# Causal masks moved from TensorE into the decay rows, another order of the query chunks, and float16 halves for part of one product

## The chip, the cores and the metric

The kernel runs on one core of a Trainium2 chip. The metric is device time in microseconds (us), as the median of three runs. A core has TensorE (PE in the profile; PEld is its weight load), VectorE (DVE), ScalarE (ACT), GpSimd (POOL) and SyncE (SP), which issues all DMAs here. Each engine takes its instructions in the order in which the program holds them, and waits on semaphores for the others.

## What is computed

Attention with a decay, then two feed-forward layers. The reference, cut:

```
scores = (1/8) * q @ k.T                           # 4 batches, 8 heads, 576 positions, 64 wide
cum    = cumsum(log(clip(f, 1e-4, 1)))
scores = where(causal, -1e9, scores + cum[:, None] - cum[None, :])
attn   = softmax(scores) @ v                       # -> x, 2304 tokens x 512
h = x @ w_in;   x = (h * sigmoid(h)) @ w_out       # layer 1, 512 -> 2048 -> 512
h = x @ w2_in;  x = (h * cos(h)) @ w2_out          # layer 2, the same sizes
```

Layer 1's `(g @ w_out)` is the "second product" below.

## The kernel before

**Tiling.** Tokens go through the layers in nine blocks of 256 (`NB`), the hidden width in eight pairs of 128 (`NPR`). One (layer, block, pair) is a step. Layer 1 takes 72 steps, layer 2 another 72. A step is 24 matmuls of the first product (tile `h`, line 1086), an elementwise chain, and the second product (tile `y`; line 1186 in layer 1 with 24 matmuls, line 989 in layer 2 with 21). Every product is computed from operands split into a high and a low half, with three matmuls of halves (`PASS`) for one full one. `h` takes float16 halves, scaled by a power of two for each operand; layer 1's `y` takes halves in fp32r (the 32-bit format that TensorE rounds), without scales; layer 2's `y` takes scaled float16 halves.

**Attention.** Positions 0 to 255 are done by 16 jobs of kind `a` (unit `c01`), positions 256 to 575 by 16 jobs of kind `b` with three units: `c2` (rows 256 to 383, 384 keys wide), `c3` (rows 384 to 511, 512 wide) and `T` (the last 64 rows of both heads, 576 wide). A unit computes its scores in PSUM (`f_s`), adds the decay row and takes the row maximum on VectorE (`top`, line 649: one operation adds the row to the scores, scales by -1/8 and keeps the minimum), exponentiates on ScalarE, normalises, transposes on TensorE (line 686) and ends in one value product for the job (line 766). The decay rows (`jb.dk`, one copy of a head's row in all 128 partitions, and `jb.dt` for `T`) come by DMA. The causal mask of a diagonal chunk is a matmul with the identity that opens the accumulation: line 632 for `c2` and `c3` (two of 128x128 in each unit), line 621 for `T` (one of 128x64), line 629 for `c01`.

**Blocks and jobs.** Blocks 0 to 3 need the jobs `a`; blocks 4 to 7 the chunks `c2` and `c3` of one batch each; block 8 all the `T` rows. So the steps of blocks 0 to 3 run between the jobs `b`.

**Weights.** All weights arrive as 64-bit words and are rebuilt on GpSimd, ScalarE and VectorE (`convert`, lines 429 to 442). `w1i` is then scaled and split into float16 (`chi` and `clo`), `w1o` split into fp32r. A scale (`scale_tasks`) is the sum of squares (ACT), one addition (DVE), a matmul with one column (line 380) and four one-column operations (DVE, lines 385 to 388).

**What sets the order.** The program is not written in the order in which it runs. Every piece is a task with an engine, a modelled duration, dependencies, buffers to acquire and a key; the `Scheduler` plays a model of the engines and emits whichever ready task has the lowest key. Steps have keys near -1000 (on PE the transposes, scores and value products of attention come ahead of them), the `a` and `b` jobs 0 to about 150, layer 1's weights 4 to about 50, and layer 2's weights 150 and up. The order that comes out is fixed in the program.

Of the kernel before, what the change touches and what calls it, by code (L numbers as in the profile page):

```python
# [43 lines left out]
W2N0, W2N1 = 16, 1.4  # L44
QA, QB = 768, 1600
# [223 lines left out]
def decay_attention_silu_cos_kernel(ctx, tc, qa, qb, f, w1i, w1o, w2i, w2o, out):  # L269
# [10 lines left out]
    w2_d = {("i", c): dr.tile([128, 2, 512], F16, name=f"w2i_d{c}") for c in range(NF)}  # L280
    w2_d.update({("o", p, k): dr.tile([128, 2, 512 if k < 3 else 256], F16, name=f"w2o_d{p}_{k}") for p in range(NPR)
# [40 lines left out]
    maskt = sb.tile([128, 64], BF16, name="maskt")  # L322
# [13 lines left out]
    rg2 = sb.tile([128, NPR], F32, name="rg2")  # L336
    v2 = sb.tile([128, 2, NPR], F32, name="v2")
    vm = sb.tile([128, 4], F32, name="vm")
    ry2 = sb.tile([128, NB], F32, name="ry2")
# [28 lines left out]
    SW = lambda l, kind, p: 2 * NB + (0 if l == 1 else NPR if kind == "i" else 2 * NPR) + p  # L368
# [143 lines left out]
    def load_tasks(jb, u):  # L512
# [45 lines left out]

        def decays():
# [37 lines left out]
        if beta:  # L597
            r.append(add("SP", 1.0, decayt, [t1], key=u, dma=c_dma(0.29), name="ldd"))
        return r

    def unit_tasks(jb, kind, pos, split, rel):
# [12 lines left out]
        def f_s():  # L614
# [5 lines left out]
            if tail:  # L620
                mm(st[1][:, 256:320], identb, maskt, start=True, stop=False, skip_group_check=True)
                for n, (x, y) in enumerate(PASS):
                    mm(st[0][:, 0:256], jb.tail[x], jb.k[y][:, 0:256], start=n == 0, stop=n == 2, skip_group_check=True)  # L623
                    mm(st[1][:, 0:320], jb.tail[x], jb.k[y][:, 256:S], start=False, stop=n == 2, skip_group_check=True)  # L624
                return
            for a in range(2):
                if kind == "c01":
# [3 lines left out]
                else:  # L631
                    mm(st[a][:, w - 128:w], identb, mask, start=True, stop=False, skip_group_check=True)
            if kind == "c01":
# [8 lines left out]
            for n, (x, y) in enumerate(PASS):  # L642
                for a in range(2):
                    r = slice(64 * a, 64 * a + 64)
                    mm(st[a][:, 0:w], jb.q[x][r, c:c + 128], jb.k[y][r, 0:w], start=False, stop=n == 2, skip_group_check=True)  # L645
# [71 lines left out]
        pe = {"c01": 0.9, "c2": 0.66, "c3": 0.8, "T": 0.86}[kind]  # L717
        ts = add("PE", pe, f_s, split + [masked], key=i - 10000.0, acq=["s", "s"] + ["e"] * heads + ["su"], rel=rel, name="S")
        te = []
        for a in range(2):  # L720
            d = {"c01": 0.78, "T": (0.45, 0.52)[a]}.get(kind, c_dve(w) + 0.15)
            t = add("DVE", d, lambda a=a: f_max(a), [ts] if not (tail and a) else [ts, t], key=i + 0.1 * a, rel=["s"], name="max")
            if not tail or a:
                h = 0 if tail else a
                te.append(add("ACT", (0.9 if kind == "c01" else c_act(w) + 0.19), lambda h=h: f_exp(h), [t], key=i + 0.1 * h,
                              name="exp"))
        tr = add("DVE", 0.3, f_rec, te, key=i, name="rec")
        r = []
        for a in range(heads):
            tn = []  # L730
            for j, (o, n) in enumerate(((0, 128), (128, 256)) if kind == "c01" else ((0, w),)):
                k = 2 * a + j if kind == "c01" else a
                def nf(eng, a=a, o=o, n=n, k=k):
# [5 lines left out]
                    acq=["s"] * (2 if tail else 1) + (["pt"] if kind in ("c01", "c2") and a == 0 else []), rel=["e"],  # L739
# [56 lines left out]
    for kind, b in ORDER:  # L796
        if kind == "a":
            pos += {1: GAP4, 2: GAP8}.get(b, 0)
        for hp in range(H // 2):
# [26 lines left out]
    MK = -1000.0  # L826

# [74 lines left out]
    xready, factor, last_out = {}, {}, {}  # L902
# [32 lines left out]
    def factor_tasks(l, j, ts, key):  # L935
# [12 lines left out]
        if l == 2:  # L948
            t = add("DVE", 0.4, f2, [ts, factors2], key=key, name="sc")
            return [t] * NPR  # L950
        wts = [wready[1, "i", 2 * p][0] for p in range(NPR)]
# [92 lines left out]
    for l, j, p in order:  # L1044
# [59 lines left out]
        if l == 1:  # L1104
# [11 lines left out]
            def half(i, s=(l, j, p)):  # L1116
                if s not in g_t:
                    g_t[s] = sbt("g", [128, 2, 2 * TB], F32R)
                return g_t[s][:, i]

# [3 lines left out]
            t3 = add(**copies(lambda half=half: half(0), src, 512, ("ACT", "DVE"), half_r), deps=[t2], key=k_el, acq=["g"],  # L1124
                     name="g")
            t4 = add(**rest(lambda half=half: half(1), src, half_r, lambda half=half: half(0).bitcast(F32), 512),
# [44 lines left out]
        prev = None  # L1171
        wdeps = [t for i in range(2) for t in wready[l, "o", 2 * p + i]]
# [89 lines left out]
```

## Time and profile before

| | |
|---|---|
| device time, median of 3 runs (lowest to highest) | 983.35 us (982.35 to 983.75) |
| the profiled execution | 983.18 us, of which the span from first to last instruction is 981.3 us |
| PE busy | 955.5 us, 97% of the span |
| DVE busy | 757.2 us, 77% |
| ACT busy | 628.0 us, 64% |
| POOL busy | 123.2 us, 13% |
| mean granted TensorE clock | 0.991 |

Busy time is an average over stages: start-up with weight conversion and the `a` jobs (to about 165 us), the `b` jobs among layer 1's steps (to about 420 us), the rest of layer 1 (to about 625 us), layer 2. Matmuls overlap in the records, so the mean duration of one (about 275 ns) is not its pace; the pace is read from the chain that ended last, where a piece of 24 matmuls stands with the time from its start to the start of the next piece.

### The profile page before, as it was taken

Reading aid. Unit: us, or ns where it says so; the run is one execution under the profiler, and the core shown is the slowest. Engines: PE = TensorE matmul, PEld = TensorE weight load, DVE = VectorE, ACT = ScalarE, POOL = GpSimd, SP = SyncE. Lnnn points to the kernel's source line nnn. Section 1 sums busy time; section 2 is a strip of 40 time slices with the busy share of each in tenths; the row PEclk is TensorE's granted clock in tenths of the full one; section 3 lists DMA queues with packets and bytes.
Section 4 is the critical chain, followed back from the end, with each engine's and each line's share of the span. In section 5 each row is a group of like instructions: output and inputs, shape, how many; then the busy total and the mean of one; then the engine's idle time right before and its main releaser. Section 6 shows DMA issues by size and latency. Waiting matters only on the chain.

```text
span 981.3 us, 20944 instructions
## 1 busy us (share of the span) xinstructions
PE 955.5 (97%) x8223; PEld 826.4 (84%) x8223; DVE 757.2 (77%) x1792; ACT 628.0 (64%) x1219; POOL 123.2 (13%) x157
## 2 busy tenths in 40 slices
PE   7996899999999999999999999999999999999997
PEld 4475688887888878889999999988888888888886
DVE  4999976677879888858778742678888888878875
ACT  6896866577776768745455432676766766766663
POOL 4865320011111121200000000000000000000000
PEclk9998899999999999999999999999999999999999
DMA  8575234435566575334433338500010001000000
GB/s 305 182 267 195 92 108 154 157 118 177 174 208 186 181 224 189 102 115 146 167 125 125 108 128 255 193 23 23 23 44 23 23 23 44 1 23 1 23 22 22
DMA packets 55906, 115.27 MB, mean 117 GB/s; under 512 B 8128, under 2 KB 18368, under 8 KB 55808
## 3 DMA queue, kind: packets, MB, share of 16 engines
q1 hardware_dynamic: 55808, 113.94, 35.0%
q8 instruction: 64, 1.05, 0.4%
q14 instruction: 34, 0.28, 0.1%
HBM read 89.20 MB, written 24.72 MB: 116 GB/s over the span
## 4 chain that ended last, share of the span: by engine, by line
PE 89%; DVE 7%; issue 1%; ACT 1%; POOL 1%; POOLq 0%; DVEq 0%; ACTq 0%
PE h L1086 37%; PE y L1186 20%; PE y L989 17%; PE pv L766 4%; PE tt L686 4%; PE st L645 3%; DVE rw L438 2%; DVE w L442 1%; DVE wi L306 1%; PE st L638 1%; PE dp L584 1%; PE st L624 1%; PE st L623 1%; DVE e L649 1%; DVE wo L300 1%
## 5 line engine op out<-in xcount | busy, mean ns | idle before, releaser
L1086 PE MATMUL h<-x,wi 128*128 128x256 f16 x3456 | 412.2, 274 | 3.1 <-ACT wi L286 1.7
L1086 PEld LDWEIGHTS <-wi 128*128 128x128 f16 x3456 | 330.0, 98 | 52.7 <-issue 6.1
L1186 PE MATMUL y<-g,wo 128*128 128x256 f32 x1728 | 238.2, 290 | 4.4 <-ACT g L286 3.6
L1186 PEld LDWEIGHTS y<-g,wo 128*128 128x128 f32 x1728 | 216.4, 192 | 11.9 <-issue 6.1
L989 PE MATMUL y<-wo,g 128*128 128x256 f16 x1512 | 176.3, 273 | 0.0
L989 PEld LDWEIGHTS <-g 128*128 128x128 f16 x1512 | 148.0, 98 | 17.1
L669 ACT ACTIVATE e<-e,su 128x128 f32<-128x128 f32 (+4 forms) x144 | 82.9, 577 | 22.5 <-DVE su L649 20.8
L1135 ACT ACTIVATE t<-h,ru 128x512 f32<-128x512 f32 x72 | 49.4, 686 | 67.3 <-PE h L1086 67.1
L1111 ACT ACTIVATE t<-h,rg 128x512 f32<-128x512 f32 x72 | 49.3, 685 | 64.1 <-PE h L1086 62.7
L1158 DVE TENSOR_TENSOR g<-t,g 128x896 f16<-128x896 f32 x72 | 78.4, 1089 | 8.7 <-ACT g L1155 5.2
L649 DVE CUSTOM_DVE_ANT_0 e<-st,dk 128x256 f32<-128x256 f32 (+3 forms) x144 | 64.1, 478 | 23.8 <-PE st L645 13.4
L288 POOL TENSOR_SCALAR e<-e,su 128x128 f32<-128x128 f32 (+4 forms) x68 | 50.7, 751 | 247.5 <-DVE su L676 135.4
L1145 DVE SCALAR_TENSOR_TENSOR t<-h,rg,t 128x512 f32<-128x512 f32 x72 | 53.9, 749 | 31.8 <-ACT t L1142 31.8
L306 DVE SCALAR_TENSOR_TENSOR g<-t,rg,g 128x512 fp32r<-128x512 f32 x72 | 55.3, 769 | 28.8 <-ACT g L286 28.2
L1141 ACT ACTIVATE t<-t,ru 128x512 f32<-128x512 f32 x72 | 51.7, 718 | 39.9 <-DVE t L1138 39.9
L1114 DVE SCALAR_TENSOR_TENSOR t<-t,h 128x512 f32<-128x512 f32 x72 | 49.2, 683 | 35.0 <-ACT t L1111 34.5
L1155 ACT ACTIVATE g<-t 128x896 f16<-128x896 f32 x72 | 67.5, 938 | 5.0 <-DVE t L1151 5.0
L286 ACT ACTIVATE g<-t,rg 128x512 fp32r<-128x512 f32 x49 | 35.3, 721 | 53.3 <-PE y L1186 50.0
L1138 DVE SCALAR_TENSOR_TENSOR t<-t,ru,h 128x512 f32<-128x512 f32 x72 | 53.5, 743 | 20.4 <-ACT t L1135 19.9
L286 ACT ACTIVATE pt<-tt 128x384 f32<-128x384 f32 (+2 forms) x90 | 44.5, 518 | 23.5 <-PE tt L686 23.1
L686 PE MATMUL tt<-ident,e 128*128 128x128 f32 x384 | 55.7, 275 | 3.4 <-POOL e L288 2.8
L1142 ACT ACTIVATE t<-t,halfpi 128x512 f32<-128x512 f32 x72 | 52.0, 722 | 2.3
(128 smaller groups left out, 1146.7 us busy)
## 6 DMA issues: line engine op xcount, KB each, us to landing
rw<-w1i SPq DMA_DIRECT2D x16, 512.0 KB, 5.2
rw<-w1o SPq DMA_DIRECT2D x16, 512.0 KB, 6.8
x<-x_d SPq DMA_DIRECT2D x16, 512.0 KB, 3.9
dk<-decay_d SPq DMA_DIRECT2D x16, 512.0 KB, 4.2
raw<-w2i SPq DMA_DIRECT2D x16, 512.0 KB, 4.9
raw<-w2o SPq DMA_DIRECT2D x16, 512.0 KB, 4.4
qs<-qb SPq DMA_DIRECT2D x16, 480.0 KB, 4.6
w2o_d<-w SPq DMA_DIRECT2D x24, 256.0 KB, 2.1
```

The source lines that it names most:

```text
L286: nc.scalar.activation(dst, src, AF.Copy, scale=scale)
L306: fn=lambda: nc.vector.scalar_tensor_tensor(out(), a(), scale(), b(), ALU.mult, ALU.subtract))
L649: nc.vector.tensor_tensor_reduce(out, s, d, -0.125, first, ALU.add, ALU.min, cell["sm"][:, o:o + 1])
L669: nc.scalar.activation(x, x, AF.Exp, bias=sm[:, i:i + 1], scale=-1.0, accum_out=sm[:, 4 + i:5 + i])
L686: nc.tensor.transpose(tt[a][:, 128 * c:128 * c + 128], e[a][:, 128 * c:128 * c + 128], ident)
L989: nc.tensor.matmul(y[bank][:, 256 * half:256 * half + 256], g[:, gi, ga], w[:, wi, 256 * col:256 * col + 256], start=p == 0 and half == 0 ...
L1086: nc.tensor.matmul(h[:, i], w[:, wi, 128 * k:128 * k + 128], x[:, xi, k], start=(i == 0 and q == 0 and k == 0), stop=(i == 1 and q == 2 an ...
L1138: nc.vector.scalar_tensor_tensor(cell["t"], cell["t"], r, cell["h"], ALU.subtract, ALU.subtract)
L1145: nc.vector.scalar_tensor_tensor(cell["t"], cell["h"], r, cell["t"], ALU.mult, ALU.mult)
L1155: nc.scalar.activation(g_t[s][:, 0], cell["w"], AF.Copy)
L1158: nc.vector.tensor_tensor(g_t[s][:, 1], cell["w"], g_t[s][:, 0], ALU.subtract)
L1186: nc.tensor.matmul(y[:, e * TB:(e + 1) * TB], w[:, wi, 128 * ec:128 * ec + 128], g[:, gi, i * TB:(i + 1) * TB], start=(st and e == 0), sto ...
```

## The change

Three edits in one.

*Masks.* For `c2`, `c3` and `T` the mask matmuls go. GpSimd writes the fill value into the masked part of the decay rows themselves by `affine_select` (`hide`): for `c3` columns 384 to 511 of both heads' rows, for `T` the last 64 columns of each half, and for `c2` columns 256 to 383. The two chunks share one set of rows, and `c3` needs columns 256 to 383 whole. So the units run as `c3`, `c2`, `T`, and the select for `c2` depends on both maxima of `c3`. The small tile `maskt` and its two copies go.

*Float16 for the second product.* From block index 3 (`J16 = 3`, the fourth of nine) layer 1's `y` takes scaled float16 halves: 48 of 72 steps. The fp32r halves of `w1o` are still made for blocks 0 to 2; from them a second set is made (squares, scales per pair, `chi`, then `left` and `low` on DVE), stored to DRAM (`w1_d`) and loaded over the fp32r set in pair p once block 2's step p has been multiplied. The factors are in `f_v1` (`rg3`) and `f3` (`ry1`), which the elementwise chain and the eviction of `y` apply.

*Keys.* The new weight tasks have keys 80 to 87, behind the `a` jobs and amid the `b` jobs.

```diff
+J16, C16 = 3, 80.0
...
-        nc.gpsimd.tensor_copy(maskt[0:64], mask[0:64, 0:64])
-        nc.gpsimd.tensor_copy(maskt[64:128], mask[64:128, 64:128])
...
+        def hide(kind):
+
+            def f():
+                if kind == "T":
+                    for a in range(2):
+                        d = jb.dt[64 * a:64 * a + 64, 512:S]
+                        nc.gpsimd.affine_select(out=d, in_=d, pattern=[[-1, 64]], compare_op=ALU.is_ge, fill=NEG, base=0,
+                                                channel_multiplier=1)
+                    return
+                c = 128 * int(kind[1])
+                d = jb.dk[:, :, c:c + 128]
+                nc.gpsimd.affine_select(out=d, in_=d, pattern=[[0, 2], [-1, 128]], compare_op=ALU.is_ge, fill=NEG, base=0,
+                                        channel_multiplier=1)
+            return f
...
+            jb.masked = {"c3": [add("POOL", 0.6, hide("c3"), [t1], key=u, name="hide")],
+                         "T": [add("POOL", 0.7, hide("T"), [td], key=u, name="hide")]}
...
-                mm(st[1][:, 256:320], identb, maskt, start=True, stop=False, skip_group_check=True)
...
-                else:
-                    mm(st[a][:, w - 128:w], identb, mask, start=True, stop=False, skip_group_check=True)
...
+        if kind == "c3":
+            jb.masked["c2"] = [add("POOL", 0.6, jb.hide("c2"), tm, key=i, name="hide")]
...
-                for i, u in enumerate(("c2", "c3", "T")):
+                for i, u in enumerate(("c3", "c2", "T")):
...
+    for p in range(NPR):
+        k, key = SW(1, "o", p), C16 + p
...
+        q = [add(**squares(lambda c=c, hi=hi: hi(c), 512, sq[:, c % 2, k:k + 1]), deps=wready[1, "o", c], key=key, name="sqw")
+             for c in pair]
+        ts = scale_tasks(k, q, key, 14)
...
+                nc.vector.scalar_tensor_tensor(st["w"], hi(c), scl[:, k:k + 1], st["t"][:, 0], ALU.mult, ALU.subtract)
...
+                nc.vector.scalar_tensor_tensor(st["t"][:, 1], lo(c), scl[:, k:k + 1], st["w"], ALU.mult, ALU.add)
...
+            w1_done[c] = add("SP", 0.46, lambda st=st, c=c: nc.sync.dma_start(w1_d[c], st["t"]), [t6], key=key, rel=["w16"],
+                             dma=c_dma(0.26), name="w2d")
...
+        if j == J16:
+            for c in (2 * p, 2 * p + 1):
+                def load16(c=c):
+                    wo_t[c] = sb.tile([128, 2, 1024], F16, tag=f"wo{c}", bufs=1, name="wo")[:, :, 0:512]
+                    nc.sync.dma_start(wo_t[c], w1_d[c])
+                wready[1, "o", c] = [add("SP", 0.46, load16, [w1_done[c], out_done[J16 - 1, p]], key=k_in - 2, dma=c_dma(0.26),
+                                         name="w2l")]
```

What it does to the order of instructions is shown at three places; in the rows `st` are scores, `e` exponentials, `su` maxima and sums, `one` and `qk` the mask's identity and the queries and keys, and the numbers tell buffers apart.

TensorE, the scores of a unit `c2` before (the second of its two masks first):

```order
L632 MATMUL st_2203<-one_133 128x128
L632 LDWEIGHTS one_133
L632 MATMUL st_2204<-one_133 128x128
L645 MATMUL st_2203<-qk_1955 128x384
L645 MATMUL st_2204<-qk_1955 128x384
```


and the scores of a unit `c3`, which now comes first, after a step's `y`:

```order
L1267 MATMUL y_1550<-g_2447,wo_1725 128x256 x6
L1267 MATMUL y_1551<-g_2447,wo_1676 128x256 x6
L1267 MATMUL y_1551<-g_2447,wo_1725 128x256 x6
L662 MATMUL st_2675<-qk_2315 128x512
L662 MATMUL st_2676<-qk_2315 128x512
```


The mask's loads and matmuls are gone, and the scores follow the step's matmuls at once.

VectorE, where the last pair of `w1i` tiles is finished (`wi`), before:

```order
L306 SCALAR_TENSOR_TENSOR wi_1734<-w_1578,scl_143,wi_1734 128x512
L940 TENSOR_SCALAR rg1_145<-inv_144 128x1 x2
L306 SCALAR_TENSOR_TENSOR wi_1732<-w_1501,scl_143,wi_1732 128x512
L288 TENSOR_SCALAR xo_1765<-pv_1725 128x256
L306 SCALAR_TENSOR_TENSOR g_1759<-t_1700,rg1_145,g_1759 128x512
L649 ISA e_1776,su_1773<-st_1774,dk_1540 128x128
L649 ISA su_1773 128x1
L649 ISA e_1776,su_1773<-st_1774,dk_1540 128x256
```


and now:

```order
L308 SCALAR_TENSOR_TENSOR wi_1777<-w_1560,scl_158,wi_1777 128x512
L1180 SCALAR_TENSOR_TENSOR t_1789<-t_1789,h_1719 128x512
L308 SCALAR_TENSOR_TENSOR wi_1787<-w_1640,scl_158,wi_1787 128x512
L870 SCALAR_TENSOR_TENSOR w_1819<-wo_444,scl_158,w16_1754 128x512
L873 SCALAR_TENSOR_TENSOR w16_1745<-wo_436,scl_158,w_1771 128x512
L873 SCALAR_TENSOR_TENSOR w16_1754<-wo_444,scl_158,w_1819 128x512
L308 SCALAR_TENSOR_TENSOR g_1827<-t_1789,rg1_160,g_1827 128x512
L387 TENSOR_SCALAR inv_159<-nrm_1779 128x1
L388 TENSOR_SCALAR inv_159<-inv_159 128x1
L389 TENSOR_SCALAR scl_158<-inv_159 128x1
L390 TENSOR_SCALAR inv_159<-scl_158 128x1
```


Behind the last `wi`, where the maxima of an attention unit stood, now stand the new weight operations (lines 870 and 873) and scale chains (lines 387 to 390). The steps' own operations (`t`, `g`) keep their places; at the 20th pass of the operation that was line 1114 the order held 88 of the 160 maxima before and holds 70 now, and all 16 new weight tiles are done by then.

GpSimd, among the `b` jobs, before:

```order
L288 TENSOR_SCALAR e_2919<-e_2919,su_2915 128x384
L288 TENSOR_SCALAR e_2961<-e_2961,su_2958 128x512
L288 TENSOR_SCALAR e_3087<-e_3087,su_3084 128x384
L288 TENSOR_SCALAR e_3088<-e_3088,su_3084 128x384
L288 TENSOR_SCALAR raw_3209<-raw_3209 128x512
L288 TENSOR_SCALAR e_3326<-e_3326,su_3323 128x384
L288 TENSOR_SCALAR raw_3321<-raw_3321 128x512
```


and now:

```order
L290 TENSOR_SCALAR e_2716<-e_2716,su_2712 128x384
L567 AFFINE_SELECT dk_2633<-dk_2633 64x64 x2
L572 AFFINE_SELECT dk_2633<-dk_2633 128x2x128
L290 TENSOR_SCALAR qk_2962<-qs_2702 128x960
L290 TENSOR_SCALAR raw_2883<-raw_2883 128x512
L290 TENSOR_SCALAR e_2900<-e_2900,su_2897 128x512
L572 AFFINE_SELECT dk_2958<-dk_2958 128x2x128
```


The selects stand in one queue with the normalisations of `e` and with the conversion of layer 2's weights (`raw`).

## Rows read from the trace of the kernel before

**Rows 1.** Busy time by stretch, us; (x) counts instructions; PEclk is the granted clock.

```profile
core 0: us, PE busy (x) PEld busy (x) DVE busy (x) ACT busy (x) POOL busy (x), PEclk, DMA share, GB/s
80.00:105.00 25.00, 15.23 (x88) 12.24 (x86) 24.27 (x67) 16.21 (x37) 9.04 (x12) 0.73 0.54 197
105.00:230.00 125.00, 124.36 (x1064) 104.43 (x1065) 93.21 (x267) 85.73 (x209) 21.16 (x29) 1.00 0.42 134
230.00:420.00 190.00, 190.00 (x1609) 158.14 (x1609) 154.50 (x439) 138.34 (x304) 32.90 (x40) 1.00 0.55 174
420.00:625.00 205.00, 204.97 (x1796) 192.27 (x1797) 135.58 (x309) 92.03 (x170) 6.62 (x8) 1.00 0.47 156
625.00:975.00 350.00, 350.00 (x3211) 313.75 (x3209) 281.55 (x535) 234.26 (x336) 0.00 (x0) 1.00 0.07 25
```

**Rows 2.** Waits of PE between 105 and 975 us: total us, times, longest us.

```profile
PE tt L686 <- ACT e L286: 0.5, 2, 0.3
```

**Rows 3.** Chain that ended last, whole run: start us, us, engine, tile, line, count.

```profile
185.88 2.35 PE pv L766 x20
...
424.59 2.86 PE y L1186 x24
...
427.45 2.64 PE h L1086 x24
...
646.57 2.62 PE h L1086 x24
```

**Rows 4.** The same chain between 160 and 186 us, one attention job.

```profile
168.29 0.11 PE st L632 x2
...
168.41 0.72 PE st L645 x6
...
175.07 0.66 PE tt L686 x6
...
177.04 0.03 PE st L621
...
177.06 0.20 PE st L623
...
182.29 0.02 PE nrm L380
...
182.31 0.81 PE y L1186 x6
```

**Rows 5.** Groups by line and shape: xcount | busy us, mean ns | idle us before.

```profile
L632 PE MATMUL st<-one 128*128 128x128 bf16 x64 | 9.0, 222 | 0.0
...
L306 DVE SCALAR_TENSOR_TENSOR w<-w,scl,w 128x512 f16<-128x512 f32 x16 | 12.1, 771 | 0.0
...
L288 DVE TENSOR_SCALAR w<-w,scl 128x512 f16<-128x512 f32 x5 | 2.3, 476 | 0.0
...
L386 DVE TENSOR_SCALAR inv<-inv 128x1 int32<-128x1 int32 x42 | 6.5, 154 | 1.4
...
L311 ACT ACTIVATE junk<-w 128x512 bf16<-128x512 f32 x48 | 30.1, 626 | 23.5 <-DVE w L442 21.8 <-DVE inv L385 1.1
...
L286 ACT ACTIVATE w<-w,scl 128x512 f16<-128x512 f32 x11 | 7.5, 714 | 0.5 <-DVE scl L387 0.4
...
L649 DVE CUSTOM_DVE_ANT_0 e<-st,dk 128x512 f32<-128x512 f32 x32 | 21.1, 686 | 7.4 <-PE st L645 7.4
...
L300 DVE TENSOR_TENSOR qk<-qs,qk 128x960 fp32r<-128x960 f32 x16 | 18.4, 1150 | 2.2 <-ACT qk L286 2.2
```

**Rows 6.** PE in order of time, 95 to 99 us; idle before and its releaser in brackets.

```profile
95.69 1.05 PE L1086 MATMUL h<-x,wi 128*128 128x256 f16 x8 [1.73 <-ACT wi L286]
...
98.11 1.04 PE L1086 MATMUL h<-x,wi 128*128 128x256 f16 x4 [1.38 <-DVE wi L306]
```

**Rows 7.** DVE in order of time: the 20th pass of line 1114.

```profile
230.52 0.68 DVE L1114 SCALAR_TENSOR_TENSOR t<-t,h 128x512 f32<-128x512 f32 x1
```

**Rows 8.** One DVE line: its durations in ns, min/median/max.

```profile
L438 DVE SCALAR_TENSOR_TENSOR rw<-rw x32: 662/686/1159, 8.6 to 124.6; 128x512 int32<-128x512 int32 x32
```

**Rows 9.** One GpSimd group: the longest select.

```profile
L356 POOL TENSOR_SCALAR_AFFINE_SELECT sel<-sel 32x1024 f32<-32x1024 f32 x1 | 1.1, 1081 | 0.1
```

More of the change, by code (lines that the diff above doesn't have):

```diff
@@ L367, in decay_attention_silu_cos_kernel @@
     SX = lambda l, j: (l - 1) * NB + j
-    SW = lambda l, kind, p: 2 * NB + (0 if l == 1 else NPR if kind == "i" else 2 * NPR) + p
+    SW = lambda l, kind, p: 2 * NB + NPR * (2 * l - 2 + (kind == "o")) + p
     def scale_tasks(i, deps, key, top=15, turns=None):
@@ L620, in f_s @@
             if tail:
-                mm(st[1][:, 256:320], identb, maskt, start=True, stop=False, skip_group_check=True)
                 for n, (x, y) in enumerate(PASS):
                     mm(st[0][:, 0:256], jb.tail[x], jb.k[y][:, 0:256], start=n == 0, stop=n == 2, skip_group_check=True)
-                    mm(st[1][:, 0:320], jb.tail[x], jb.k[y][:, 256:S], start=False, stop=n == 2, skip_group_check=True)
+                    mm(st[1][:, 0:320], jb.tail[x], jb.k[y][:, 256:S], start=n == 0, stop=n == 2, skip_group_check=True)
                 return
-            for a in range(2):
-                if kind == "c01":
+            if kind == "c01":
+                for a in range(2):
                     v = st[a].rearrange("p (c s) -> p c s", c=4)
@@ L716, in unit_tasks @@
         i = pos
-        pe = {"c01": 0.9, "c2": 0.66, "c3": 0.8, "T": 0.86}[kind]
+        pe = {"c01": 0.9, "c2": 0.56, "c3": 0.7, "T": 0.86}[kind]
         ts = add("PE", pe, f_s, split + [masked], key=i - 10000.0, acq=["s", "s"] + ["e"] * heads + ["su"], rel=rel, name="S")
-        te = []
+        te, tm = [], []
         for a in range(2):
             d = {"c01": 0.78, "T": (0.45, 0.52)[a]}.get(kind, c_dve(w) + 0.15)
-            t = add("DVE", d, lambda a=a: f_max(a), [ts] if not (tail and a) else [ts, t], key=i + 0.1 * a, rel=["s"], name="max")
+            hidden = [] if kind == "c01" or tail and not a else jb.masked[kind]
+            t = add("DVE", d, lambda a=a: f_max(a), hidden + ([ts] if not (tail and a) else [ts, t]), key=i + 0.1 * a, rel=["s"],
+                    name="max")
+            tm.append(t)
             if not tail or a:
@@ L738, in unit_tasks @@
             t = add("PE", 0.115 * nb, lambda a=a: f_t(a), tn + [jb.first], key=i + 0.1 * a - 15000.0,
-                    acq=["s"] * (2 if tail else 1) + (["pt"] if kind in ("c01", "c2") and a == 0 else []), rel=["e"],
+                    acq=["s"] * (2 if tail else 1) + (["pt"] if kind in ("c01", "c3") and a == 0 else []), rel=["e"],
                     name="T")
@@ L950, in factor_tasks, with f3 @@
             return [t] * NPR
+        def f3():
+            nc.vector.tensor_scalar(ry1[:, j:j + 1], inv[:, k:k + 1], vm[:, 3:4], 2.0 ** 15, ALU.mult, ALU.mult)
+        if j >= J16:
+            ry_done[j] = add("DVE", 0.2, f3, [ts, factors1], key=key, name="sc")
         wts = [wready[1, "i", 2 * p][0] for p in range(NPR)]
@@ L1123, in decay_attention_silu_cos_kernel @@
             src = lambda cell=cell: cell["t"]
-            t3 = add(**copies(lambda half=half: half(0), src, 512, ("ACT", "DVE"), half_r), deps=[t2], key=k_el, acq=["g"],
+            t3 = add(**copies(lambda half=half: half(0), src, 512, ("ACT", "DVE"), out_r),
+                     deps=[t2, factors1 if j >= J16 else None], key=k_el, acq=["g"],
                      name="g")
-            t4 = add(**rest(lambda half=half: half(1), src, half_r, lambda half=half: half(0).bitcast(F32), 512),
+            t4 = add(**rest(lambda half=half: half(1), src, out_r, whole, 512),
                      deps=[t3], key=k_el, rel=["t"], name="gl")
```

54 lines of the change are left out of this document (44 added, 10 removed).

## The prediction

> **What bounds the kernel now.** I read the busy time by stretch first. From 105 us to the end of the span PE is busy for 124.36 of 125 us, then 190.00 of 190, 204.97 of 205 and 350.00 of 350, at a granted clock of 1.00 [rows 1]. The view of waits says the same from the other side: the largest wait of PE between 105 and 975 us is 0.5 us in total, in two pieces [rows 2]. So TensorE is the bound for 870 of 981 us, and the chain of waits [rows 3] is there simply PE's instructions in order; each piece's duration in it is the pace at which PE works. A microsecond of PE work that goes after 105 us shortens the kernel by one, as long as the other engines keep their places. Before 105 us it is different: in 80 to 105 us PE is busy for 15.23 of 25 us, DVE for 24.27, and the granted clock is 0.73 [rows 1]; there PE waits for converted weights (1.73 us for `wi` from ACT, 1.38 us for `wi` from DVE) [rows 6]. That row is also the picture of what a full DVE would do later.
>
> The second thing to read is what is left free: DVE has 125 − 93.2 = 31.8 us free in 105 to 230 us, 35.5 in 230 to 420 and 69.4 in 420 to 625; ACT has 39.3 and 51.7 us free in the first two [rows 1].
>
> **Float16 second product.** A `y` piece of 24 matmuls with fp32r halves takes 2.86 us on the chain, 119.2 ns a matmul. The `h` of layer 2, 24 matmuls of 128x256 of float16 halves among float16 neighbours, takes 2.62 us, 109.2 ns. Same shape, so the changed `y` should take 2.62: 0.24 us for each of 48 steps, 11.5 us. The `h` beside an fp32r `y` takes 2.64, 0.02 more than in layer 2 [rows 3]; if that is the change of type, another 48 × 0.02 = 1.0. I take **12.5 us**; without the second and with 0.02 of the first lost to rounding it is 48 × 0.22 = 10.6, the lower end.
>
> **Masks.** Sixteen jobs lose two mask matmuls in `c2`, two in `c3` and one in `T`. The group at line 632 has 64 of them [rows 5]. Their own mean of 222 ns is a record of overlapping matmuls; on the chain a pair takes 0.11 us and `T`'s single one 0.03 [rows 4]. The row of the pair is the first of 32 such on the whole chain, which add up to 4.58 us, 0.14 on the mean; with 16 × 0.04 for `T` that is 5.2 us at most. It can be less: a mask also covers the weight load of the first score matmul, and where `T`'s mask goes ahead the three or six behind it may open slower. A first matmul that waits for its load would cost about the 0.20 − 0.12 = 0.08 us by which `T`'s first row [rows 4] exceeds an average matmul of its size; 48 units × 0.08 = 3.8 leave 1.4 us. The new order of TensorE puts other matmuls straight ahead of the scores, which hide a load just as the mask did, so I take **4.5 us** (1.4 to 5.2).
>
> **Scale chains on PE.** Eight new scales bring eight one-column matmuls: 0.02 us each, and the six `y` matmuls behind one took 0.81 us [rows 4], where six at 119.2 ns take 0.715. So 0.12 each, **1.0 us lost**.
>
> **The new weight work on DVE and ACT.** This is the price that no row shows directly. Sixteen tiles take two operations each on DVE, of the form of line 306 (771 ns): 24.7 us. Five of the sixteen roundings `chi` stand on DVE (476 ns): 2.4. Eight scale chains have five small operations each, by 154 ns: 6.2; the factors `f_v1`, five more: 0.8 [rows 5]. Together 34 us on DVE. ACT gets 16 squares (626 ns) and 11 roundings (714 ns) [rows 5], 18 us. In the new order all of it lies between about the fourth step and the 20th pass of the `t` operation, which before stood at 230.5 us [rows 7]. DVE had 31.8 us free in 105 to 230 us [rows 1], so on the face of it 34 do not fit. The order makes room: by that pass it holds 70 maxima where it held 88, that is three `b` jobs fewer. A job is about 6.7 us of PE work: scores 0.72 us for 6 × 384 columns, so 2.2 for all three units; 19 transposes at 0.11, 2.1; a value product of 2.35 [rows 3, 4]. So PE gets to that pass 20 us sooner, after 105 us instead of 125, and DVE loses with each job six maxima (686 ns at 512 columns) and a subtraction on `q` and `k` (1.15 us) [rows 5], 5 us a job at least and about 7 with evictions and normalisations: 15 to 21. DVE then has 93 + 34 − (15 to 21) = 106 to 112 us of work by these means for 105 us of PE work. Durations taken from a mean count twice what overlaps between neighbours, so I put it at 100 to 110: **full or nearly so**. A DVE that is a few us behind does not stop PE at once: `y` runs two steps behind `h`, and attention work whose inputs are ready stands between. And since the new tiles are wanted only from block four, they are placed where the order had the maxima of jobs that are not needed yet. I take **2.5 us** of new idle on PE there, with 0 and 10 as ends: the upper is DVE's excess of 7 plus two waits of the kind of rows 6 (1.4 to 1.7 us).
>
> A rule of the Trainium skill bears on this. What the trace shows: line 438, a DVE operation with two SBUF inputs, takes 686 ns at the median and up to 1159 in the start-up, where GpSimd works beside it [rows 8]. The page "SBUF — State Buffer", section "Who interferes with whom", says that DVE's second port pair is GpSimd's too and is held exclusively, so that an instruction of one waits for the other's. By that rule each of the 64 new selects could hold up one DVE operation.
>
> **The selects on GpSimd.** POOL is busy for 21 of 125 us and 33 of 190 us [rows 1]. It gets 64 instructions in 48 tasks: 32 of 128 x 256 (`c3` and `c2`) and 32 of 64 x 64 (`T`). The one large select of the trace, 32 partitions of 1024, took 1.08 us [rows 9], which is an upper end for both by columns: 32 × 1.08 + 32 × 1.08 = 69 us at the very most, 20 at a quarter of it for the smaller; spread over 315 us with 54 busy, they fit. If each held up a DVE operation by 1159 − 686 = 0.47 us [rows 8], DVE would have 64 × 0.47 = 30 us more over the whole of the `b` jobs, 67 us free in two stretches [rows 1]; it bears on the sum only where DVE is already full, in the stretch above, and there for some 25 selects or 12 us: this is part of the first rival. The selects of `c3` and `T` need only the decay rows and stand well ahead of the maxima. Those of `c2` come behind `c3`'s maxima and ahead of `c2`'s; a job's maxima of `c2` wait for two hand-overs and one select (1 to 1.5 us), while the steps' own DVE operations stand between in the order.
>
> **Edits at nothing.** The two `maskt` copies on POOL lie in the start-up, where PE waits for weights [rows 6]; at most 1 us comes of it. The 16 stores and 16 loads of 256 KB are issued by SP; the queues move 0.42 to 0.55 of what they can [rows 1]. A load over `w1o`'s fp32r pair p is released by block index 2's step p and wanted eight steps later, about 8 × 5.5 = 44 us on PE [rows 3]; if it is queued behind another load it still has that long. Layer 2 has the same work in the same order.
>
> **The sum.** 12.5 + 4.5 − 1.0 − 2.5 = 13.5 us off the profiled execution's 983.18 gives 969.7. Its own time is 0.17 below the median of the three runs, so **969.9 us** against 983.35.
>
> **Rivals.** *DVE becomes the bound between 105 and 210 us.* For: the sum of 106 to 112 us for 105, the 12 us of possible hold-ups by selects, and 80 to 105 us, where a full DVE left PE 39% idle at a lower clock [rows 1]. Against: the attention jobs can slip, and layer 2's weight work has 69 us free behind [rows 1]. Price: PE idles 5 to 14 us instead of 2.5, so 972 to 981.
> *The selects for `c2` come late and the kernel gets slower.* Each of the 16 jobs makes `c2`'s first maximum wait on DVE for GpSimd; DVE is in order, so the `t` and `g` operations of the next step wait behind it, and TensorE for these. With a wait of d in each job, DVE loses 16 d; it has 35.5 us free in 230 to 420 us [rows 1], so PE is hit from d = 2.2 us on. With gains of 16 us, the kernel is slower by over 0.2% when 16 d − 35.5 is above 18, so from d = 3.35 us; at 3.7 it gives 983.35 − 16 + 23.7 = 991. The normalisations of `e`, which share POOL's queue, speak for a wait, its low load against one as long as this.
> *Float16 `y` does not run faster,* because something else than the type sets 119.2 ns (the eviction, or the weight load). Then only the masks are left: 983.35 − 4.5 + 3.5 = 982.4. Against it speak layer 2's 109.2 ns with the same tiles [rows 3].
>
> **How the numbers follow.** Forecast 0.70, between 966 (no idle, masks at 5.2) and 972. DVE as the bound 0.22, 972 to 981. Slower through the selects 0.05. No gain by type 0.03. The range 964.5 to 978 holds the forecast and two thirds of the first rival. A measurement of this kernel can tell 0.2%, 2 us: the first rival stays faster by that in all but its last hundredth or two, so faster 0.90, same 0.05, slower 0.05.
>
> **What the profile after should show.** The chain has `y` x24 with 2.86 in block indices 0 to 2 and 2.62 from 3 on, `h` with 2.62 beside it. Lines 632 and 621's mask matmuls are gone, and a job's scores take 0.72 for `c2` as before. PE's idle time from 105 us to the 20th pass of `t` is 2 to 3 us, DVE is above 90% busy there, and that pass comes about 20 us sooner. DVE's waits for POOL's selects are small. The prediction is wrong if `y` stays at 2.86, if PE's waits for `g` from DVE or ACT add up to 5 us or more, or if DVE waits for `dk` from POOL for more than 2 us a job.

## The result, and the profile after

The changed kernel takes 958.22 us (median of 4 runs, 957.8 to 958.88) against 983.12 us (4 runs), a ratio of 0.9748 with a 95% interval of 0.9731 to 0.9765. That is 24.9 us less, where 13.5 were forecast, and below the range. The profiled execution took 957.8 us, with a span of 956.0.

The changed kernel's busy time by stretch, same columns as [rows 1]; PE does the same work sooner, so the later stretches begin earlier:

```profile
core 0: us, PE busy (x) PEld busy (x) DVE busy (x) ACT busy (x) POOL busy (x), PEclk, DMA share, GB/s
80.00:105.00 25.00, 19.03 (x146) 16.38 (x146) 24.69 (x64) 22.83 (x55) 11.86 (x10) 0.86 0.67 239
105.00:230.00 125.00, 124.96 (x1076) 107.59 (x1074) 114.02 (x330) 90.36 (x222) 28.42 (x41) 1.00 0.53 171
230.00:400.00 170.00, 170.00 (x1466) 137.22 (x1465) 150.78 (x420) 127.38 (x278) 48.04 (x82) 1.00 0.63 206
400.00:605.00 205.00, 205.00 (x1871) 180.04 (x1872) 142.15 (x352) 115.50 (x222) 13.76 (x20) 1.00 0.51 168
605.00:950.00 345.00, 344.81 (x3163) 308.82 (x3160) 278.66 (x528) 230.50 (x329) 0.00 (x0) 1.00 0.07 23
```

TensorE is still the bound, and from 105 us on it has no idle time to speak of: 0.04 us up to 230 us. VectorE did fill up there, from 93.2 to 114.0 us of 125, without TensorE waiting for it. The surprise stands in the first line: 80 to 105 us, which I had taken to stay as it was, has PE busy for 19.03 us and not 15.23, at a granted clock of 0.86 and not 0.73 [rows 1].

The chain that ended last in the changed kernel (start us, us, piece) shows layer 1's `y` at float16's pace, as forecast; it took 2.86 [rows 3]:

```profile
446.35 2.62 PE y L1267 x24
448.96 2.62 PE h L1152 x24
```

What the new work costs on its own engines, by line and shape (count | busy us, mean ns | idle before), first the two operations of the new weight set on DVE, then the selects on POOL:

```profile
L870 DVE SCALAR_TENSOR_TENSOR w<-wo,scl,w 128x512 f32<-128x512 f32 x16 | 12.2, 768 | 0.0
L873 DVE SCALAR_TENSOR_TENSOR w<-wo,scl,w 128x512 f16<-128x512 f32 x16 | 12.1, 766 | 0.1
```

```profile
L572 POOL TENSOR_SCALAR_AFFINE_SELECT dk<-dk 128x256 f32<-128x256 f32 x32 | 21.1, 665 | 59.4 <-DVE su L666 44.8 <-DMA dk<-decay_d 7.4 <-DVE inv L387 7.1
L567 POOL TENSOR_SCALAR_AFFINE_SELECT dk<-dk 64x64 f32<-64x64 f32 x32 | 11.8, 369 | 21.9 <-DMA dk<-decay_d 20.9
```

The DVE operations cost what the nearest row had said (771 ns) [rows 5]; the selects take 33 us in all. VectorE's only wait for a select, in its view of waits (total us, times, longest):

```profile
DVE e L666 <- POOL dk L572: 0.3, 1, 0.3
```

### The profile page after: what moved, and what is told of

Read it like the earlier page. It is cut to its first block, busy times and chain, and to the rows that moved or that the text cites. A ratio compares the mean times of both kernels' runs of the same rounds, so it can differ in the third digit from the quotient of the medians.

```text
span 956.0 us, 21150 instructions
## 1 busy us (share of the span) xinstructions
PE 933.0 (98%) x8153; PEld 794.6 (83%) x8153; DVE 779.5 (82%) x1867; ACT 648.8 (68%) x1273; POOL 155.1 (16%) x221
## 4 chain that ended last, share of the span: by engine, by line
PE 90%; DVE 7%; issue 1%; ACT 1%; DMA 0%; POOL 0%; DVEq 0%; POOLq 0%; ACTq 0%
PE h L1152 38%; PE y L1267 20%; PE y L1055 17%; PE pv L788 5%; PE tt L703 4%; PE st L662 3%; DVE rw L440 1%; DVE w L444 1%; PE st L655 1%; DVE wo L302 1%; DVE wi L308 1%; PE dp L602 1%; PE st L644 1%; PE st L643 1%; DVE e L666 1%
## 5 line engine op out<-in xcount | busy, mean ns | idle before, releaser
L1267 PE MATMUL y<-g,wo 128*128 128x256 f16 (+1 forms) x1728 | 219.9, 280 | 1.4 <-ACT g L288 0.8
L1267 PEld LDWEIGHTS <-wo 128*128 128x128 f16 x1152 | 110.6, 98 | 15.3 <-issue 2.2
L1267 PEld LDWEIGHTS y<-g,wo 128*128 128x128 f32 x576 | 74.2, 196 | 7.0 <-issue 3.5
L308 DVE SCALAR_TENSOR_TENSOR g<-t,rg,g 128x512 f16<-128x512 f32 (+1 forms) x72 | 56.3, 782 | 25.8 <-ACT g L288 25.4
L288 ACT ACTIVATE g<-t,rg 128x512 f16<-128x512 f32 (+1 forms) x54 | 38.9, 721 | 54.7 <-PE y L1267 54.6
L666 DVE CUSTOM_DVE_ANT_0 e<-st,dk 128x256 f32<-128x256 f32 (+3 forms) x144 | 64.3, 478 | 14.3 <-PE st L662 6.7
L290 POOL TENSOR_SCALAR e<-e,su 128x512 f32<-128x512 f32 (+4 forms) x67 | 46.9, 705 | 159.1 <-DVE su L693 61.7
```

Source lines behind the costliest of these rows:

```text
L288: nc.scalar.activation(dst, src, AF.Copy, scale=scale)
L308: fn=lambda: nc.vector.scalar_tensor_tensor(out(), a(), scale(), b(), ALU.mult, ALU.subtract))
L666: nc.vector.tensor_tensor_reduce(out, s, d, -0.125, first, ALU.add, ALU.min, cell["sm"][:, o:o + 1])
L1267: nc.tensor.matmul(y[:, e * TB:(e + 1) * TB], w[:, wi, 128 * ec:128 * ec + 128], g[:, gi, i * TB:(i + 1) * TB], start=(st and e == 0), sto ...
```

## What the two traces say side by side

**Masks.** In the timeline of PE (start us, us, operation, count) of the kernel before, the job of [rows 4] reads:

```profile
162.99 0.96 PE L1186 MATMUL y<-g,wo 128*128 128x256 f32 x6
163.79 0.49 PE L686 MATMUL tt<-ident,e 128*128 128x128 f32 x3
...
168.13 0.28 PE L632 MATMUL st<-one 128*128 128x128 bf16 x2
168.34 0.79 PE L645 MATMUL st<-qk 64*128 64x384 f32 x6
169.06 1.92 PE L1086 MATMUL h<-x,wi 128*128 128x256 f16 x16
...
182.14 0.18 PE L380 MATMUL nrm<-sq,ones 128*128 128x1 bf16 x1
182.18 0.95 PE L1186 MATMUL y<-g,wo 128*128 128x256 f32 x6
182.97 1.05 PE L1086 MATMUL h<-x,wi 128*128 128x256 f16 x8
```

The mask pair starts at 168.13, the scores behind it at 168.34: 0.21 us, where the chain gives the pair 0.11 [rows 4]. The chain starts a piece when the one before has been drained, so part of a changeover is booked on the neighbour; from start to start nothing is left over. Summed in this way the 64 matmuls of line 632 take 6.74 us and the 16 of line 621 0.51, 7.2 us in all, and the scores take as long after the change as before (14.35 and 14.38 us for the 96 of 512 columns, 11.56 both times for those of 384).

**y.** In the same rows six fp32r matmuls of `y` take 0.80 us from start to start (162.99 to 163.79), with no one-column matmul ahead of them. Behind one they take 0.79 (182.18 to 182.97), and the one-column matmul itself takes 0.04. So the 0.81 of [rows 4] that I charged to the scale chain is the price of a `y` that is cut into sixes. The same piece in the changed kernel, 0.66 us:

```profile
344.69 0.82 PE L1267 MATMUL y<-g,wo 128*128 128x256 f16 x6
345.35 0.17 PE L382 MATMUL nrm<-sq,ones 128*128 128x1 bf16 x1
```

Over all `y` from block index 3 on, start to start, the kernel before has 124.9 ns a matmul and the changed one 109.9: 17.2 us for 1152. `h` gives some back (108.4 to 109.5 ns after 105 us, 3.4 us). Most of this is a matter of where a changeover is booked, not a slower `h`: in the kernel before, an uncut `h` ahead of an fp32r `y` has 2.55 us from its start to the start of `y` (427.30 to 429.85 in the rows at the end), and in the changed kernel 2.62, that is 0.07 more for each of 48 steps, 3.4 us. In that piece of the kernel before the last `h` matmul has 28 ns to the start of `y`, and the first `y` matmul has 202 ns instead of about 120. So `h` and `y` have to be taken together: uncut, the pair takes 5.50 us before and 5.24 after, 0.26 less.

**Start-up.** PE's waits between 15 and 105 us (total us, times, longest) were, before:

```profile
PE y L1186 <- ACT g L286: 3.6, 1, 3.6
PE tt L686 <- POOL e L288: 2.6, 4, 0.9
PE nrm L380 <- DVE sq L376: 2.1, 1, 2.1
PE h L1086 <- ACT wi L286: 1.7, 1, 1.7
PE h L1086 <- DVE wi L306: 1.4, 1, 1.4
```

and in the changed kernel:

```profile
PE tt L703 <- POOL e L290: 4.0, 5, 1.2
PE nrm L382 <- DVE su L666: 2.0, 1, 2.0
PE nrm L382 <- DVE sq L378: 1.2, 1, 1.2
PE nrm L382 <- DVE inv L387: 1.1, 1, 1.1
PE y L1267 <- ACT g L288: 0.8, 1, 0.8
```

The 3.6 us for `g` and both waits for `wi` are gone or small; others are new or longer, so that of PE's idle time between 15 and 120 us, 13.0 us, 10.2 are left. The granted clock of 80 to 105 us rose as well, from 0.73 to 0.86. The program order says why this can be: from the 171st matmul of the traces on, the changed kernel has another order. Before, 90 `h` and 54 `y` matmuls stand among the first 144 of both; after, 72 and 72. The planner had reordered the start because there are new tasks in it, not because a step there changed.

So three candidates stand for the missing 11 us: masks, a dearer cut `y`, and the start-up. The experiments take them one by one. All ran five rounds beside the kernel before, whose median was 982.88 to 982.97 us in each of the three sets.

## The experiments

**Masks alone.** In these diffs `NB` is 9, so no block uses float16.

```diff
-J16, C16 = 3, 80.0
+J16, C16 = 9, 80.0
...
-    for p in range(NPR):
+    for p in range(NPR if J16 < NB else 0):
...
-    factors1 = add("DVE", 0.9, f_v1, sc1 + ...
+    factors1 = None if J16 == NB else add("DVE", 0.9, f_v1, sc1 + ...
```

> Only the masks move into the decay rows and the chunks run as c3, c2, T; layer 1's second product stays fp32r everywhere and no second weight set is made. In the program order TensorE's first 950 matmuls are those of the kernel before. Theory A (a mask pair costs what lies between the start of its piece and the start of the next: 0.22 us, and 0.03 for T's): 32 x 0.22 + 16 x 0.03 = 7.5 us less, ratio 0.9924, and the start-up as before. Theory B (the prediction's term, the piece as the chain draws it, 0.14 us): 4.5 to 5.2 us less, ratio 0.995. Theory C (the start-up's gain came with the masks): 11 us less, ratio 0.989.

Measured: 975.73 us, 7.2 less than before, ratio 0.9928 (0.9915 to 0.9940). Theory A; the chain's 4.5 to 5.2 us is too low. Its start-up is that of the kernel before:

```profile
80.00:105.00 25.00, 15.23 (x89) 12.39 (x88) 24.27 (x67) 16.64 (x37) 8.25 (x12) 0.73 0.55 196
```

**Order alone.**

```diff
-                for i, u in enumerate(("c2", "c3", "T")):
+                for i, u in enumerate(("c3", "c2", "T")):
```

> The kernel before with the chunks run as c3, c2, T and nothing else: mask matmuls and fp32r as before. Theory A (the masks' 7.2 us are the mask matmuls alone): ratio 1.000, within 1 us. Theory B (part of it is the order, which puts the 512 wide scores first): 2 to 3 us less, ratio 0.9975.

Measured: 982.03 us, ratio 0.9992 (0.9983 to 1.0001), no change that can be told. The 7.2 us are the mask matmuls.

**Mask matmuls doubled.**

```diff
                     mm(st[a][:, w - 128:w], identb, mask, start=True, stop=False, skip_group_check=True)
+                    mm(st[a][:, w - 128:w], identb, mask, start=False, stop=False, skip_group_check=True)
```

> The kernel before with each of the 64 mask matmuls of c2 and c3 issued twice in a row (the masked scores only get a more negative value). Theory A (of a pair's 0.22 us, 0.11 is streaming 2 x 128 columns, and as much again is paid once for changing to the identity and back): the second ones cost 64 x 0.056 = 3.6 us, ratio 1.0036. Theory B (each mask matmul costs 0.11 by itself): 7.0 us more, ratio 1.007. If they were hidden under weight loads: no change.

Measured: 985.5 us, 2.6 more, ratio 1.0033 (1.0021 to 1.0046, which is 2.1 to 4.5 us): theory A. Its timeline of PE around one `c2`:

```profile
167.03 0.22 PE L632 MATMUL st<-one 128*128 128x128 bf16 x1
167.08 0.22 PE L633 MATMUL st<-one 128*128 128x128 bf16 x1
167.14 0.22 PE L632 MATMUL st<-one 128*128 128x128 bf16 x1
167.20 0.22 PE L633 MATMUL st<-one 128*128 128x128 bf16 x1
167.34 0.79 PE L646 MATMUL st<-qk 64*128 64x384 f32 x6
```

The masks start 0.05 to 0.06 us apart, and from the last one to the scores it is 0.14. So of a pair's 0.21 us only 0.11 is streaming; the rest is the changeover behind it, which is paid once however many masks there are. The page "TensorE: Matmul & The Clock Gate" of the Trainium skill, section "Back-to-back issue gap", gives an isolated matmul of 128 columns about 56 ns and a stream of load and matmul pairs of that size about 81; this trace agrees with the first, although a weight load stands ahead of each mask in the program.

**Float16 alone.** The mask matmuls, `maskt` and the order `c2`, `c3`, `T` are put back into the changed kernel:

```diff
-                for i, u in enumerate(("c3", "c2", "T")):
+                for i, u in enumerate(("c2", "c3", "T")):
...
+                for a in range(2):
+                    mm(st[a][:, w - 128:w], identb, mask, start=True, stop=False, skip_group_check=True)
...
-            hidden = [] if kind == "c01" or tail and not a else jb.masked[kind]
+            hidden = []
```

> Only float16 from block index 3 with its weight work; mask matmuls, chunk order c2, c3, T and constant masks as before. Theory A (y from start to start 122.8 ns against 108.4, 16.6 us for 48 steps, of which h gives back 2.7; and 4 us of the start-up, whose order of the first matmuls this edit changes): 17 to 18 us less, ratio 0.982. Theory B (the prediction's terms: 12.5 for the pieces, 1.0 and 2.5 lost to the new work): 9 us less, ratio 0.991. Without the start-up's gain but with the pieces by start to start: 14 us, ratio 0.986.

Measured: 965.24 us, 17.7 less, ratio 0.9820 (0.9806 to 0.9833). With the masks' 7.2 that makes 24.9, the whole. So the edits add up, and the start-up comes with this one. (Added up matmul by matmul, the 16.6 us of theory A for `y` are 17.2 and the 2.7 of `h` are 3.4; what is left of them, 13.8, hardly differs.)

**The set made, not used.** `J16 = 9` alone, so that the loop over the pairs still runs:

```diff
-J16, C16 = 3, 80.0
+J16, C16 = 9, 80.0
```

> The changed kernel's masks, and the second weight set made and stored, but never used: fp32r in all nine blocks. TensorE's first matmuls stand as in the changed kernel. Against the run with the masks alone it shows what making the set costs or brings. Theory A (the work is hidden, and the start-up's other order brings 4 us): 4 us faster than masks alone, ratio about 0.988. Theory B (the work costs 2.5 to 3.5 us of PE's time): slower than masks alone by that, ratio 0.998.

Measured: 972.53 us, ratio 0.9895 (0.9879 to 0.9910), 3.2 us **faster** than the masks alone, with only work added. To the changed kernel it is 14.3 us: that is what the use of float16 brings.

**The same in the kernel before.** The float16-alone kernel with `J16 = 9`.

> The kernel before, with the second weight set made and stored and never used; masks, chunk order and fp32r as before. It has only work added. Theory A (34 us of DVE and 18 us of ACT work are hidden, and the order of the first steps that comes with the added tasks brings about 4 us): 3 to 4 us less than before, ratio 0.996. Theory B (added work costs): 2.5 to 3.5 us more, ratio 1.003.

Measured: 980.67 us, 2.3 less, ratio 0.9975 (0.9966 to 0.9985). Theory A in sign, but less than its 3 to 4 us: the interval is 1.5 to 3.3. The squares of the new set fill holes of ACT early, as one row of its timeline (start us, us) shows:

```profile
77.13 0.63 ACT L313 ACTIVATE junk<-wo 128x512 bf16<-128x512 f32 x1
```

**The start-up put back.** The set is made, but its squares wait for the last converted weights:

```diff
-        q = [add(**squares(lambda c=c, hi=hi: hi(c), 512, sq[:, c % 2, k:k + 1]), deps=wready[1, "o", c], key=key, name="sqw")
+        q = [add(**squares(lambda c=c, hi=hi: hi(c), 512, sq[:, c % 2, k:k + 1]), deps=wready[1, "o", c] + wready[1, "o", 15] + wready[1, "i", 15], key=key, name="sqw")
```

> As the run with the second weight set made and not used, but its squares wait until all of w1i and w1o has been converted, so that they cannot fill holes of ACT in the start-up; TensorE's first 717 matmuls then stand as in the kernel before. The set is still made, stored and unused, and the masks lie in the decay rows. Theory A (the 3.2 us between 'set unused' and 'masks alone' are the other order of the start-up): they are gone, time as with the masks alone, 975.7 us, at most 1 us more, ratio 0.9925. Theory B (they come from somewhere else in the added work): time stays at 972.5, ratio 0.9895.

Measured: 976.25 us, ratio 0.9934 (0.9922 to 0.9946): the gain is gone, and the row of 80 to 105 us is that of before again:

```profile
80.00:105.00 25.00, 15.19 (x89) 12.30 (x87) 24.27 (x67) 16.47 (x37) 9.26 (x12) 0.73 0.56 195
```

With the squares free (the set made, not used) that row read:

```profile
80.00:105.00 25.00, 18.03 (x134) 15.15 (x134) 24.62 (x67) 21.66 (x51) 11.28 (x11) 0.86 0.64 229
```

All other work of the new set hangs on its squares, so the run holds that back too. Over the whole of the stretch the two rows are, first with the masks alone, then with the set made and not used:

```profile
15.00:120.00 105.00, 91.98 (x657) 63.45 (x654) 98.98 (x268) 82.08 (x224) 59.86 (x71) 0.93 0.56 196
15.00:120.00 105.00, 93.85 (x694) 67.15 (x691) 100.09 (x270) 90.21 (x250) 62.51 (x72) 0.97 0.57 197
```

PE idles 1.9 us less and has a higher granted clock, 0.97 instead of 0.93. So the 3.2 us are not waits alone; no run here parts the waits from the clock.

The run with the squares held also shows what making the set costs where the start-up is the same: 976.25 − 975.73 = 0.5 us, within what can be told from nothing.

**The same with float16 in use,** the changed kernel with the squares held.

> The changed kernel, whole, but the squares of the new weight set wait for the end of the conversion, so TensorE's first 717 matmuls stand as in the kernel before. Theory A (3.2 us of the changed kernel's gain are the other start-up): 958.2 + 3.2 = 961.4 us, up to 1 us more, ratio 0.978. Theory B (the start-up does not carry over once float16 is used): 958.2, ratio 0.9748.

Measured: 964.59 us, ratio 0.9815 (0.9802 to 0.9829), 6.3 us above the changed kernel and not 3.2. At least half is the start-up: between 15 and 120 us PE idles 12.1 us where the changed kernel idles 10.2, and in 80 to 105 us its granted clock is 0.68 and not 0.86. For the rest this kernel's rows show PE idle where the changed kernel's PE is not:

```profile
80.00:105.00 25.00, 15.69 (x88) 12.79 (x87) 24.14 (x67) 17.25 (x40) 9.10 (x12) 0.68 0.56 194
105.00:180.00 75.00, 74.82 (x647) 63.51 (x645) 67.93 (x215) 54.17 (x151) 15.86 (x23) 0.99 0.36 111
180.00:250.00 70.00, 69.28 (x591) 59.71 (x590) 66.92 (x166) 49.43 (x105) 21.02 (x31) 1.00 0.76 241
250.00:400.00 150.00, 148.56 (x1281) 119.56 (x1279) 130.30 (x360) 113.10 (x247) 50.91 (x75) 1.00 0.65 209
```

0.18 + 0.72 + 1.44 = 2.3 us between 105 and 400 us, with DVE at 96% in 180 to 250 us, against 90% in the changed kernel. The view of waits has two there, both of the one-column matmul of a scale chain for DVE, 1.4 and 0.7 us. It looks like the first rival in small, the weight work that was held back meeting a DVE that is full, which the changed kernel is spared because its squares were done early. That is argued and not shown: with the same work held back and float16 unused, DVE was as full in 180 to 250 us (66.48 of 70) and PE idled for 0.2 us there.

**Float16 from block index 6.**

```diff
-J16, C16 = 3, 80.0
+J16, C16 = 6, 80.0
```

> The changed kernel with float16 from block index 6 instead of 3: 24 steps, all behind the last attention job but for a few, where h and y stand as unbroken 24s. Theory A (the gain of a step hangs on how often its y is cut into pieces: an h and y uncut takes 5.50 us before and 5.24 after, one cut in sixes loses 0.14 us for each six): 24 x 0.26 = 6.2 us below 'set unused', 966.3 us, ratio 0.983, and blocks 3 to 5 then hold the other 8 us of the 14.3. Theory B (the same gain in each step): 7.2 us, 965.4 us, ratio 0.982.

Measured: 966.94 us (965.77 to 967.94), ratio 0.9838 (0.9825 to 0.9852). Against "made, not used" the last 24 steps bring 5.6 us, 0.23 a step; the 24 steps of blocks 3 to 5, among the attention jobs, then bring 8.7, 0.36 a step. That speaks for theory A, a `y` that attention cuts gains more, but the two forecasts lie only 0.9 us apart, and the cutting is the smaller part of the difference. Added up from start to start, `h` and `y` of blocks 6 to 8 take 6.7 us less than in "made, not used" (0.28 a step), and those of blocks 3 to 5 then 7.8 us less (0.32 a step): about 1 us of the 3.1. PE's idle time up to 620 us differs by more: 11.3 us in "made, not used", 12.5 here, 10.2 in the changed kernel.

**Float16 from block index 2,** with the new weights' key at 60.

```diff
-J16, C16 = 3, 80.0
+J16, C16 = 2, 60.0
```

> The changed kernel with float16 from block index 2 (56 steps instead of 48) and the new weight work 20 units earlier in the planner's keys. Theory A (each of the eight steps more saves what blocks 3 to 5 saved, 8.7 / 24 = 0.36 us, and DVE keeps up): 2.9 us below the changed kernel, 955.3 us, ratio 0.972. Theory B (DVE, at over 90% between 105 and 230 us, is late with the new weights): 1 to 5 us above the changed kernel, ratio 0.976 to 0.980.

Measured: 957.81 us, ratio 0.9747 (0.9734 to 0.9760): as the changed kernel, neither theory. Block 2's `y` did get cheaper, 25.1 to 21.4 us from start to start. But PE is busy for 18.08 and not 19.03 of 25 us in 80 to 105 us and idles 0.8 us longer up to 120 us; `h` has 109.9 instead of 109.5 ns after 105 us, 1.6 us; and the scores there take 46.1 us instead of 45.2. So the gain is given back in three places. Of `h`'s 1.6 us, 8 × 0.07 = 0.6 are the changeovers that were booked on `y` before; the rest is not settled.

**The same with the key at 40.**

```diff
-J16, C16 = 3, 80.0
+J16, C16 = 2, 40.0
```

> As the run before it, float16 from block index 2, with the new weight work another 20 units earlier (key 40, level with the a jobs). Theory A (the earlier work is hidden too): as that run, 955 us, ratio 0.972. Theory B (it now competes with layer 1's conversion in the start-up): 2 to 6 us above that run.

Measured: 966.76 us, ratio 0.9835 (0.9822 to 0.9849), 9 us above the run before it. The stretch of 105 to 180 us, and PE's four largest waits in it:

```profile
105.00:180.00 75.00, 69.15 (x583) 59.42 (x583) 69.50 (x201) 52.42 (x129) 9.11 (x12) 0.98 0.48 154
```

```profile
PE nrm L382 <- DVE inv L387: 1.4, 2, 1.1
PE st L649 <- DVE inv L387: 1.2, 2, 0.8
PE tt L703 <- POOL e L290: 0.9, 1, 0.9
PE st L649 <- DVE su L666: 0.7, 1, 0.7
```

PE is idle for 5.85 of 75 us, where with the key at 60 it idles for none. Its one-column matmul of the scale chains and the scores of a late `a` job wait for small operations of DVE; in PE's queue the steps' matmuls stand behind them. DVE is hardly busier than in the changed kernel (69.50 us against 68.57 in the same stretch, where PE is busy for all 75). So it is not the share of DVE that tells the two apart; that the place of the new work in its queue does is the likely cause, not shown by itself.

**Each select issued twice,** in `hide`, for example:

```diff
-                nc.gpsimd.affine_select(out=d, in_=d, pattern=[[0, 2], [-1, 128]], compare_op=ALU.is_ge, fill=NEG, base=0,
-                                        channel_multiplier=1)
+                for _ in range(2):
+                    nc.gpsimd.affine_select(out=d, in_=d, pattern=[[0, 2], [-1, 128]], compare_op=ALU.is_ge, fill=NEG, base=0,
+                                            channel_multiplier=1)
```

> The changed kernel with each of the 64 selects issued twice in a row (the second changes nothing). By the changed kernel's trace they take 665 ns (128 x 256) and 369 ns (64 x 64), so GpSimd gets 33 us more. Theory A (they are off the path): time as the changed kernel, within 0.5 us, ratio 0.975. Theory B (each holds up VectorE or a maximum by 0.3 to 0.5 us, where VectorE is nearly full): 5 us or more above it, ratio 0.980.

Measured: 959.61 us, ratio 0.9764 (0.9751 to 0.9778): 1.4 us above the changed kernel, intervals overlapping, so between the theories and nearer to A. VectorE's waits for a select grew from 0.3 to 2.2 us, three of them. The two operations of the new set take 768 and 766 ns in the mean in the changed kernel; with twice the selects their medians stay where they were (744 and 747 ns against 747 and 747), and DVE's busy time over the whole span grows from 779.5 to 784.6 us for 64 more selects, 0.08 each. The prediction had allowed 0.47 us each [rows 8]; here a select costs DVE about a sixth of that. The Trainium skill's page "SBUF — State Buffer", section "Who interferes with whom", makes the port pair that DVE and GpSimd share an exclusive lock. This run does not contradict it; but 5.1 us would be 11 holds of 0.47 us, not 64.

## Why the prediction was wrong

The sign, the bound and both mechanisms were right; the sum was short by 11.4 us, and the range did not reach the time. By its terms:

| term | forecast, us | measured, us | from |
|---|---|---|---|
| masks | −4.5 (1.4 to 5.2 less) | −7.2 | masks alone |
| float16 `y` | −12.5 | −14.3 | changed kernel against "made, not used" |
| making the set: its scale chains on PE, idle time of PE | +1.0 and +2.5 (0 to 10) | −3.2 | "made, not used" against masks alone |
| sum | −13.5 | −24.7 | whole: −24.9 |

- **What bounds the kernel: right.** PE is busy for all but 0.2 us from 105 to 950 us, and each microsecond of its work that went is in the time.
- **Masks: the size failed,** and the upper end with it. I took the piece in the chain, 0.11 to 0.14 us, as what a pair costs; from start to start it is 0.21. The doubled masks show the difference as a changeover of about 0.1 us that goes with the pair. My reason for less, that a mask hides the load of the first score, has no support: the scores take the same time without it.
- **Float16: mechanism right, size 1.8 us short.** `y` takes 2.62 us from block index 3 on, as said, and for an uncut step the term comes out: 0.26 us for `h` and `y` together, as 12.5/48. Its parts do not: from start to start `y` gains 0.33, and the `h` beside it does not lose 0.02 but has 0.07 more. What was left out is the cutting: among the attention jobs `y` comes in pieces, and six fp32r matmuls take 0.80 us where six at 2.86/24 would take 0.715. The row with 0.81 was in my hands [rows 4], and I read it as the cost of the one-column matmul ahead. That loss of 1.0 us does not exist: that matmul takes 0.04, and all eight new ones 0.4 us in the run with the squares held against the masks alone.
- **DVE and the start-up: wrong in sign.** DVE's load was put at 100 to 110 for 105 us; in 105 to 210 us it was 97.0, and PE did not wait. That the added work could bring a gain was left out, since the bounds of that term began at nothing. The new squares entered ACT's holes, the planner turned the first steps around, and 3.2 us went away in the stretch whose waits and low clock I had shown in [rows 1, 6]. I had compared the order of the changed kernel only where the new operations stand; its first 144 matmuls of the steps would have shown another order at the very stretch in which PE waits. That does not tell which way it goes: the gain is luck of the order, and a term there needed both signs.
- **The pass of `t`** that was to come some 20 us sooner came at 203.7 us and not 230.5: 27 sooner, of which the start-up's gain is a part.
- **Selects: right.** They wait for `c3`'s maxima, not the other way round; VectorE waited for one for 0.3 us in all, so the slower rival had no ground. They take 33 us on GpSimd; the 69 us given as the most holds, and the 20 does not come out of its row (a quarter of 1.08 us for all 64 is 17). **The first rival** did not come about here. Waits of PE for DVE of its kind came two steps away: 2.3 us with held squares, and about 6 with a key of 40 and eight more steps.
- **The third rival,** that float16 would not run faster, is refuted by 2.62 us.

What stays open: how the start-up's gain divides between waits and clock, how much of the gain of blocks 3 to 5 is the cutting, and where about 1 us of `h` goes with float16 from block index 2.

## What to carry to other kernels

Price matmuls that go or change from start to start in the timeline, over the pieces as they really stand, changeovers included, and not from the best unbroken piece or from a piece's share of the chain; and count the neighbour with them, since a changeover can be booked on either side. Where a planner sets the order, look at the program order in every stretch in which the bounding engine waits, also far from the edit: added tasks alone moved this kernel by 3 us, and a term of either sign belongs there. A nearly full second engine need not cost anything, but a key set 20 units too early cost 9 us.

## What the runs showed of the hardware

- Two 128-column mask matmuls hold TensorE for 0.21 us between other matmuls, and two more in the same place add only 0.08 to 0.11 (2.6 us for 32 pairs; 0.05 to 0.06 us apart): the changeover is as dear as the work.
- An fp32r product of 24 matmuls pays for being cut: 0.80 us for six against 2.95 for 24 from start to start, 133 against 123 ns each. In float16 it is 0.66 and 2.62, 109 each, where the piece stands between `h`, transposes and one-column matmuls; next to scores or value products six take up to 0.76. In the kernel before:

```profile
424.35 3.11 PE L1186 MATMUL y<-g,wo 128*128 128x256 f32 x24
427.30 2.79 PE L1086 MATMUL h<-x,wi 128*128 128x256 f16 x24
429.85 3.11 PE L1186 MATMUL y<-g,wo 128*128 128x256 f32 x24
```

- A GpSimd select's time does not follow its columns: 369 ns for 64 x 64, 665 ns for 128 x 256, and 292 ns for the one of 128 x 128 that makes the identity in the same trace.
